# Two 64-row matmul passes in place of the last tail pass of the gate chain and of the up chain

## The chip, the cores and the metric

The kernel runs on one NeuronCore of a Trainium2 chip. The metric is the device time of one execution in microseconds. Inside the core five engines work from queues of their own: TensorE (PE in the profile, with its weight loads as PEld), VectorE (DVE), ScalarE (ACT), GpSimd (POOL) and SyncE (SP). PE, DVE and ACT each take their instructions strictly in the order in which the program wrote them, and wait on each other through semaphores. Matmuls read SBUF and write PSUM; ScalarE and VectorE read PSUM.

## The reference

The inputs are a matrix x of 2048 tokens by 576 features and the weights of two branches. A gate per token mixes the branches.

```python
g = sigmoid((x * gate_w).sum(-1, keepdims=True))
a = irfft2(rfft2(x) * (w_r + 1j * w_i))               # spectral branch, 2048 x 576
b = (gelu(x @ w_gate) * (x @ w_up)) @ w_down          # GEGLU branch, 576 -> 4608 -> 576
out = g * a + (1 - g) * b
```

All is float32. The kernel gets float32 accuracy out of faster matmuls by splitting each operand in a high part of 12 bits of mantissa and a low part, the rest. A product is then three passes: high by high, low weights by high x, high weights by low x.

## The kernel before, in words

**Two streams of work.** The GEGLU branch is the stream that feeds TensorE. The spectral branch is a long list of VectorE and ScalarE work (Python generators in the list `gens`), of which a piece is written into the program at every call of `gap()`, as far as a credit allows; `tick(us)` raises the credit by the time of the matmuls just written. So the order on each engine is fixed when the program is built.

**Slots.** In the first part of the program, tokens come in blocks of 512 (`tb`), and the 4608 hidden features in 36 tiles of 128 (`j`). A slot is one pair of hidden tiles for one token block: `hidden(j)`, then two calls of `down` for the slot before, then `hidden(j + 1)`, whose `mid` holds the other two calls of `down`. The next slot starts with its `hidden` at once; nothing is written on PE between the second `hidden` of a slot and the first `hidden` of the next.

**One hidden tile.** `hidden` calls `chain` twice: the gate chain into one PSUM buffer, then the up chain into the other. `pgu` is the name of these buffers, and `ps_gu()` hands out two of them in turn, so every gate chain uses the same buffer as the gate chain before it. A chain is 14 matmuls of 128 rows by 512 columns. The 576 features are four full blocks of 128 (three passes each, L728 to L730, from `xhi` and `xlo`) and a tail of 64. The tail's weights stand twice in the 128 rows; in `xtl` rows 0 to 63 hold the high part of the tail of x and rows 64 to 127 the low part, so L734 (high weights) does high by high and high by low in one pass, and L735 (low weights) does low by high and low by low.

After the gate chain ScalarE computes the GELU out of PSUM (L766, into `gl`), while PE runs the up chain. Then VectorE multiplies by the up chain's PSUM (L770), ScalarE makes the high part of the hidden tile (`hb`, L213) and VectorE the low part (L775). `down` reads `hb` a slot later with 128 by 288 matmuls (L789); ScalarE empties their PSUM (`pdn`) into `stg` (L814), and a DMA adds it to `yd`.

**The start.** The first hidden tile is written by `first_chains` (L747), which follows the arrival of x and the weights; the GELU after it is L763. `prep_x(tb, 4, src)` makes `xtl`: a ScalarE copy, then two VectorE steps (`stacked`, L217 and L218), the first of which overwrites `src`.

Of the kernel before, what the change touches and what calls it, by code (L numbers as in the profile page):

```python
# [10 lines left out]
F32 = mybir.dt.float32  # L11
F32R = mybir.dt.float32r
AF = mybir.ActivationFunctionType
ALU = mybir.AluOpType

P = 128
# [9 lines left out]
TB = 512  # L26
# [132 lines left out]
def _build(nc, tc, a):  # L159
    with ExitStack() as ctx:  # L160
        ctx.enter_context(tc.manual_schedule())
        pool = ctx.enter_context(tc.tile_pool(name="sb", bufs=1))
# [5 lines left out]
        def mk(n, shape, dt=F32):  # L168
            return pool.tile([P] + shape, dt, name=n, tag=n)
# [13 lines left out]
        raw = [raws[:, i * (KT * 256 + D):(i + 1) * (KT * 256 + D)] for i in range(2)]  # L183
        hb = [mk(f"hb{i}", [2, TB], F32R) for i in range(3)]
        gl = [mk(f"gl{i}", [TB]) for i in range(2)]
        xraw = mk("xraw", [4, TB])
        stg = [mk(f"stg{i}", [2, HD]) for i in range(4)]
        gs = mk("gs", [NB])
        gate = mk("gate", [NB])
# [22 lines left out]
        def copy(o, i):  # L212
            act.activation(o, i, AF.Copy)  # L213

        def stacked(o, x):

            vec.tensor_scalar(x, x, msk[:, 1:2], None, op0=ALU.mult)  # L217
            vec.scalar_tensor_tensor(o, f(o), msk[:, 0:1], x, op0=ALU.mult, op1=ALU.add)  # L218
# [11 lines left out]
        def columns():  # L230
# [4 lines left out]
            sgn = tmp[:, 3 * SW:3 * SW + NK]  # L235
            turn = [d + 4 * q for d in range(4) for q in range(4)]
            Z = [st[q] for q in turn]
            flat = xraw.rearrange("p q k -> p (q k)")
            sp, gw, xg = flat[:, 0:SW], flat[:, SW:SW + D], flat[:, 1280:1280 + D]
            xh2, xl2, vs2 = two(xh), two(xl), two(vs)  # L240

# [162 lines left out]
        def first_tiles(h):  # L404

            sp = tmp[:, 0:2 * SW].rearrange("p (e k) -> p e k", e=2)
            tmps = [tmp[:, SW * i:SW * (i + 1)] for i in range(4)]
            tmps = [(x, x[:, 0:NK], x[:, NK:]) for x in tmps]
            e = slice(2 * h, 2 * h + 2)
            yield from _butterfly(vec, lambda i: T[:, i, e], lambda i: T[:, i, e, re], lambda i: T[:, i, e, im],  # L410
                                  TAKEN, sp, -1, (1.37, 0.76))
            places = [((k, TAKEN[o]), o * k) for k in range(1, 4) for o in range(1, 4) if TAKEN[o] // 2 == h]
            yield from _twiddles(vec, act, lambda d, e: T[:, d, e], lambda d, e: T[:, d, e, re],
                                 lambda d, e: T[:, d, e, im], places, tmps, -1, 0.5)
            yield None
# [181 lines left out]
        def spectral(rows):  # L597
            yield from forward_rows(0, rows)
            rows = rows_tile()
            load_rows(rows, 1)  # L600
            zero_pads(0)
            yield None
            yield from first_tiles(0)
            yield None
            zero_pads(1)
            yield from forward_rows(1, rows)
            for _ in range(3):
                yield None
            yield from first_tiles(1)
            yield from columns()  # L610
            yield from last_tiles()
            for h in range(2):
                yield from inverse_rows(h)
# [3 lines left out]
        aux = []  # L617
        later = []
        gens = []
        side = []  # L620
        credit = [0.0]
        count = [0]

        def tick(us):
            credit[0] += RATE * us
# [52 lines left out]
        def prep_x(tb, k, src):  # L678
            if k < 4:
                copy(xhi[tb][:, k], src)  # L680
                vec.tensor_tensor(xlo[tb][:, k], src, f(xhi[tb][:, k]), ALU.subtract)
                credit[0] -= 0.7
            else:
                copy(xtl[tb], src)
                stacked(xtl[tb], src)
                credit[0] -= 1.45

# [32 lines left out]
            copy(g[:, 0], r)  # L720
            lower(("dn", j), g, r, 0.76)

        def chain(j, s, tb):
            due(("gu", j))
            ps, w = ps_gu(), gu[j % 3]
            c = slice(s * P, (s + 1) * P)
            for k in range(4):
                pe.matmul(ps, w[:, 0, k, c], xhi[tb][:, k], start=k == 0, stop=False)  # L728
                pe.matmul(ps, w[:, 1, k, c], xhi[tb][:, k], start=False, stop=False)  # L729
                pe.matmul(ps, w[:, 0, k, c], xlo[tb][:, k], start=False, stop=False)  # L730
                tick(3 * 0.2265)
                if k in (0, 2):
                    gap()
            pe.matmul(ps, w[:, 0, 4, c], xtl[tb], start=False, stop=False)  # L734
            pe.matmul(ps, w[:, 1, 4, c], xtl[tb], start=False, stop=True)  # L735
            tick(2 * 0.2265)
            return ps

        def first_chains():

# [15 lines left out]
        def hidden(j, tb, mid):  # L756

            i = hn[0]
            hn[0] += 1
            g, h = gl[i % 2], hb[i % 3]  # L760
            if i == 0:
                pg, pu = first_chains()
                act.activation(g, pg, AF.Gelu_apprx_tanh)  # L763
            else:
                pg = chain(j, 0, tb)
                act.activation(g, pg, AF.Gelu_apprx_tanh)  # L766
                mid()
                pu = chain(j, 1, tb)
            def mult():
                vec.tensor_tensor(g, g, pu, ALU.mult)  # L770
                credit[0] -= 0.7
                copy(h[:, 0], g)

            def low():
                vec.tensor_tensor(h[:, 1], g, f(h[:, 0]), ALU.subtract)  # L775
                credit[0] -= 0.7

            seq(("h", i), (1, mult), (3, low))
            return h, ("h", i)
# [86 lines left out]

        def load_xs(i):
            for q in range(4):
                nc.sync.dma_start(xraw[:, q], a["xs"][q // 2, q % 2][:, i])

        def operands():

            sx = pool.tile([P, 16 * SW], F32R, name="sx", tag="til")
            s4 = pool.tile([P, 2 * UNIT], F32R, name="s4", tag="tmp")
            parts = [sx[:, 2048 * i:2048 * (i + 1)].rearrange("p (l t k) -> p l t k", l=2, t=2) for i in range(3)]
            parts.append(s4[:, 0:2048].rearrange("p (l t k) -> p l t k", l=2, t=2))
            tails = [sx[:, 6144 + TB * i:6144 + TB * (i + 1)] for i in range(6)] + [s4[:, 2048:2560]]
            for i in range(4):
                ops["s1 s2 s3 s4".split()[i]] = (parts[i][:, 0], parts[i][:, 1], tails[i])
            ops["a11"] = (xhi[0][:, 0:2], xlo[0][:, 0:2], tails[4])  # L880
            ops["a12"] = (xhi[0][:, 2:4], xlo[0][:, 2:4], tails[5])
            ops["a22"] = (xhi[1][:, 2:4], xlo[1][:, 2:4], tails[6])
            m = misc[:, 0:TB]
            for i in range(3):
                if i:
                    load_xs(i)
                    for _ in range(6):
                        yield None
                a11, a12, a21, a22 = (xraw[:, q] for q in range(4))
                if i == 2:  # L890
                    for n, x in (("a11", a11), ("a12", a12), ("a22", a22)):
                        tail_of(ops[n][2], x)
                        yield 1.4
                        yield None
                for o, x, z, op in ((m, a21, a22, ALU.add), (a21, a11, a21, ALU.subtract),
                                    (a11, m, a11, ALU.subtract), (a12, a12, a11, ALU.subtract)):
                    vec.tensor_tensor(o, x, z, op)
                    yield 0.72
                sums = (("s1", m), ("s2", a11), ("s3", a21), ("s4", a12))
                yield None  # L900
                if i == 2:
                    for n, x in sums:
                        tail_of(ops[n][2], x)
                        yield 1.4
                        yield None
                else:
                    for n, x in sums:
                        copy(ops[n][0][:, i], x)
                    yield None
                    yield None  # L910
                    for n, x in sums:
                        vec.tensor_tensor(ops[n][1][:, i], x, f(ops[n][0][:, i]), ALU.subtract)
                        yield 0.72
            ops["done"] = True
# [58 lines left out]
        def products(i, spare, pend):  # L973

            j = NT + 2 * i
            u, c, u3 = gl, [xraw[:, q] for q in range(2)], [xraw[:, q] for q in range(2, 4)]
            made = {}

            def finish(name, x):
# [102 lines left out]
        ps = ps_gu()  # L1082
# [32 lines left out]
        def load_x(i):  # L1115
            if i < 2 * KT:
                tb, k = divmod(i, KT)
                nc.sync.dma_start(xraw[:, i % 4], a["xt"][1][:, k, tb * TB:(tb + 1) * TB])

        def reload_x(tb):  # L1120
            for k in range(KT):
                i = KT * tb + k
                aux.append(lambda i=i, k=k: [prep_x(tb, k, xraw[:, i % 4]), load_x(i + 4)])

        NBLK = NT // 2
        prev = None
# [124 lines left out]
```

## Time and profile before

| what | value |
|---|---|
| median of 3 runs | 1380.88 us (1380.46 to 1381.74) |
| the profiled execution, its own time | 1381.8 us |
| its span, first to last instruction | 1380.0 us |
| PE busy | 1370.2 us, 99% of the span |
| DVE, ACT, POOL busy | 1108.8, 687.1 and 269.6 us |
| mean granted TensorE clock | 0.999 |

The profile is one execution. Its page gives for each engine the busy time, groups of instructions by source line, the digits of 40 slices of the span, and the chain of work that ended last. Other views list instructions in order of time (start, duration, engine, line, operation, tiles; in brackets the idle time of the engine just before, and what ended it), or the busy time in chosen stretches. A matmul's row shows 0.39 us for a 512-column pass although the next begins 0.22 to 0.23 us later: passes are pipelined, and the start-to-start distance is what one costs.

### The profile page before, as it was taken

How to read it: one execution, taken by the hardware profiler on the slowest of the kernel's cores; microseconds unless marked ns; L12 is line 12 of the kernel's file. 1: busy time of each engine (PE TensorE's matmuls, PEld its weight loads, DVE VectorE, ACT ScalarE, POOL GpSimd, SP SyncE). 2: the span in 40 equal slices, each digit the busy share in tenths (PEclk: the TensorE clock that was granted, in tenths of full speed). 3: DMA queues.
4: the chain of work that ended last, by engine and by line, in shares of the span. 5: the costliest groups of instructions: out<-in, count | busy, mean ns of one | idle time of the engine just before them, and what ended most of it. 6: DMA issues, size and time to landing. Idle time of an engine off the chain costs nothing.

```text
span 1380.0 us, 19978 instructions
## 1 busy us (share of the span) xinstructions
PE 1370.2 (99%) x7518; PEld 1211.3 (88%) x7518; DVE 1108.8 (80%) x1628; ACT 687.1 (50%) x1051; POOL 269.6 (20%) x326
## 2 busy tenths in 40 slices
PE   8999999999999999999999999999999999999998
PEld 6888888888888898888888888888888888888887
DVE  5999789888968787678989898857877777777776
ACT  4553443544465565554354634375555555555552
POOL 0022121222222222211111311232111111111110
PEclk9999999999999999999999999999999999999999
DMA  7466676666899999765675576687677777776776
GB/s 265 143 124 112 122 158 122 115 111 139 205 224 261 234 230 243 145 121 105 143 149 137 120 155 138 111 207 152 126 130 131 129 130 130 130 128 128 131 155 172
DMA packets 97041, 210.91 MB, mean 153 GB/s; under 512 B 11824, under 2 KB 22064, under 8 KB 96560
## 3 DMA queue, kind: packets, MB, share of 16 engines
q0 software_dynamic: 45248, 92.56, 44.0%
q1 hardware_dynamic: 51696, 117.08, 27.6%
q8 instruction: 59, 0.97, 0.3%
q14 instruction: 38, 0.31, 0.1%
HBM read 110.43 MB, written 92.01 MB: 147 GB/s over the span
## 4 chain that ended last, share of the span: by engine, by line
PE 96%; DVE 2%; DMA 1%; issue 0%; ACT 0%; SPq 0%; DVEq 0%
PE pdn L789 32%; PE pgu L728 12%; PE pgu L730 12%; PE pgu L729 12%; PE pgu L966 3%; PE pgu L968 3%; PE pgu L967 3%; PE pgu L735 3%; PE pgu L734 3%; PE pone L966 2%; PE pone L968 2%; PE pone L967 2%; PE pf L275 2%; PE pgu L969 2%; PE pone L969 1%; DVE tmp L661 1%
## 5 line engine op out<-in xcount | busy, mean ns | idle before, releaser
L802 POOL DMA_DIRECT2D yd<-stg x264 | 230.9, 878 | 996.5 <-ACT stg L814 880.6
L789 PEld LDWEIGHTS pdn<-dn,hb 128*128 128x128 f32 x2856 | 395.0, 188 | 11.6 <-DVE raws L843 0.5
L789 PE MATMUL pdn<-dn,hb 128*128 128x288 f32 x2856 | 403.1, 295 | 0.2 <-DVE raws L843 0.2
L814 ACT ACTIVATE stg<-pdn,omg 128x576 f32<-128x576 f32 x272 | 201.6, 743 | 402.4 <-PE pdn L789 312.6
L728 PE MATMUL pgu<-xhi,gu 128*128 128x512 f32 x760 | 297.8, 392 | 2.7 <-ACT gl L763 2.1
L730 PE MATMUL pgu<-xlo,gu 128*128 128x512 f32 x760 | 297.1, 391 | 0.0
L729 PE MATMUL pgu<-xhi,gu 128*128 128x512 f32 x760 | 296.9, 391 | 0.0
L730 PEld LDWEIGHTS pgu<-xlo,gu 128*128 128x128 f32 x760 | 143.0, 188 | 31.1
L728 PEld LDWEIGHTS pgu<-xhi,gu 128*128 128x128 f32 x760 | 143.1, 188 | 29.9 <-ACT gl L763 2.5
L729 PEld LDWEIGHTS pgu<-xhi,gu 128*128 128x128 f32 x760 | 143.0, 188 | 25.7
L770 DVE TENSOR_TENSOR gl<-gl,pgu 128x512 f32<-128x512 f32 x96 | 65.8, 685 | 73.1 <-PE pgu L735 72.6
L213 ACT ACTIVATE hb<-gl 128x512 fp32r<-128x512 f32 x96 | 60.2, 627 | 114.1 <-DVE gl L770 114.0
L766 ACT ACTIVATE gl<-pgu 128x512 f32<-128x512 f32 x95 | 56.8, 598 | 90.9 <-PE pgu L735 90.8
L213 ACT ACTIVATE gu<-raws 128x1280 fp32r<-128x1280 f32 (+3 forms) x83 | 87.0, 1048 | 5.0 <-DMA raws<-wgu 4.8
L775 DVE TENSOR_TENSOR hb<-gl,hb 128x512 fp32r<-128x512 f32 x96 | 65.9, 686 | 18.4 <-ACT hb L213 18.3
L789 PEld LDWEIGHTS pdn<-dn,gu 128*128 128x128 f32 x576 | 79.0, 188 | 1.8
L789 PE MATMUL pdn<-dn,gu 128*128 128x288 f32 x576 | 80.1, 295 | 0.0
L735 PE MATMUL pgu<-xtl,gu 128*128 128x512 f32 x190 | 74.0, 389 | 0.0
L734 PE MATMUL pgu<-xtl,gu 128*128 128x512 f32 x190 | 73.9, 389 | 0.0
L708 DVE TENSOR_TENSOR gu<-raws,gu 128x1280 fp32r<-128x1280 f32 x46 | 68.3, 1484 | 3.9 <-ACT gu L213 3.8
L708 DVE TENSOR_TENSOR dn<-raws,dn 128x576 fp32r<-128x576 f32 x72 | 54.1, 751 | 1.3 <-ACT dn L213 1.3
L984 DVE TENSOR_TENSOR xraw<-xraw 128x512 f32<-128x512 f32 x48 | 33.2, 693 | 26.4 <-ACT xraw L992 25.9
(213 smaller groups left out, 2109.9 us busy)
## 6 DMA issues: line engine op xcount, KB each, us to landing
yd<-stg POOLq DMA_DIRECT2D x264, 288.0 KB, 5.1
raws<-wgu SPq DMA_DIRECT2D x46, 640.0 KB, 5.0
raws<-wd SPq DMA_DIRECT2D x72, 288.0 KB, 2.8
colm<-col POOLq DMA_DIRECT2D x32, 256.0 KB, 6.1
quads<-ws SPq DMA_DIRECT2D x20, 384.0 KB, 4.6
raws<-ws SPq DMA_DIRECT2D x18, 384.0 KB, 4.8
tmp<-wf SPq DMA_DIRECT2D x16, 290.0 KB, 5.8
cns<-til SPq DMA_DIRECT2D x64, 72.5 KB, 5.2
```

Of the source, the lines that this page charges most:

```text
L213: act.activation(o, i, AF.Copy)
L708: vec.tensor_tensor(g[:, 1], r, f(g[:, 0]), ALU.subtract)
L728: pe.matmul(ps, w[:, 0, k, c], xhi[tb][:, k], start=k == 0, stop=False)
L729: pe.matmul(ps, w[:, 1, k, c], xhi[tb][:, k], start=False, stop=False)
L730: pe.matmul(ps, w[:, 0, k, c], xlo[tb][:, k], start=False, stop=False)
L734: pe.matmul(ps, w[:, 0, 4, c], xtl[tb], start=False, stop=False)
L735: pe.matmul(ps, w[:, 1, 4, c], xtl[tb], start=False, stop=True)
L789: pe.matmul(ps[half], h[:, l, c], d[:, q, half * HD:(half + 1) * HD], start=part == 0 and n == 0, stop=part == 1 and n == 2)
L802: pl.dma_start(yd[u], o, accum_op=ALU.add)
L814: put(u, lambda o: act.activation(o.rearrange("p (c k) -> p c k", c=2), v[:, :, 0:HD], AF.Copy, scale=omg[:, u:u + 1]), i == 0)
L966: pe.matmul(ps, hi[:, c], xh[:, t], start=t == 0, stop=False)
L967: pe.matmul(ps, lo[:, c], xh[:, t], start=False, stop=False)
```

## The change

While a flag `twin` is set, both chains leave out their last pass (the low tail weights). When the up chain is done, `last_halves` writes two matmuls of 64 rows each: rows 0 to 63 of the low tail weights of the gate, with the high part of x in rows 0 to 63 of `xtl`, into the gate's PSUM buffer; and rows 64 to 127 of the low tail weights of the up projection, with a copy of the high part of x in rows 64 to 127 of a new tile `xth`, into the up buffer. The two use different rows of the array and different PSUM buffers. The products of low weights by low x, which L735 also computed, are left out where the flag is set.

The GELU is now written after these two passes, because the gate's PSUM sum is complete only then. `prep_x` gets one more ScalarE copy (64 rows) for each of the two token blocks. The credit of a chain is smaller by half a pass. `xth` takes the memory of `xraw`, which is allocated later, at the start of `columns`. The flag is cleared when the spectral stream reaches `first_tiles(1)`. In the built program the new line (L750 of the changed file) stands 66 times: 33 hidden tiles have it, the second tile of the first slot and both tiles of the 16 slots after that; 17 of these are the second tile of a slot and 16 the first.

```diff
@@ prep_x
                 copy(xtl[tb], src)
+                if twin[0]:
+                    copy(xth[64:128, tb], src[64:128])
                 stacked(xtl[tb], src)
@@ chain
-        def chain(j, s, tb):
+        def chain(j, s, tb, whole):
...
             pe.matmul(ps, w[:, 0, 4, c], xtl[tb], start=False, stop=False)
-            pe.matmul(ps, w[:, 1, 4, c], xtl[tb], start=False, stop=True)
-            tick(2 * 0.2265)
+            if whole:
+                pe.matmul(ps, w[:, 1, 4, c], xtl[tb], start=False, stop=True)
+            tick((1.5 + 0.5 * whole) * 0.2265)
             return ps
+
+        def last_halves(j, tb, ps):
+
+            for s, x in enumerate((xtl[tb], xth[:, tb])):
+                r = slice(64 * s, 64 * s + 64)
+                pe.matmul(ps[s], gu[j % 3][r, 1, 4, s * P:(s + 1) * P], x[r], start=False, stop=True)
@@ hidden
-                pg = chain(j, 0, tb)
-                act.activation(g, pg, AF.Gelu_apprx_tanh)
+                halves = twin[0]
+                pg = chain(j, 0, tb, not halves)
+                if not halves:
+                    act.activation(g, pg, AF.Gelu_apprx_tanh)
                 mid()
-                pu = chain(j, 1, tb)
+                pu = chain(j, 1, tb, not halves)
+                if halves:
+                    last_halves(j, tb, (pg, pu))
+                    act.activation(g, pg, AF.Gelu_apprx_tanh)
+
@@ spectral
+            twin[0] = False
             yield from first_tiles(1)
```

Two places show what moves. The first is PE at the end of a slot's second hidden tile and the start of the next slot. `xtl_71` and `xtl_70` are the tails of the two token blocks, `gu_75` and `gu_76` two buffers of split gate and up weights; the brackets name the engine whose semaphore the instruction waits on. Before:

```order
L730 MATMUL pgu<-xlo_69,gu_75 128x512
L734 MATMUL pgu<-xtl_71,gu_75 128x512
L735 MATMUL pgu<-xtl_71,gu_75 128x512
L728 MATMUL pgu<-xhi_66,gu_76 128x512 [waits Activation_49]
L729 MATMUL pgu<-xhi_66,gu_76 128x512 [waits DVE_49]
```

And with the change:

```order
L736 MATMUL pgu<-xlo_69,gu_75 128x512
L740 MATMUL pgu<-xtl_71,gu_75 128x512
L750 MATMUL pgu<-xtl_71,gu_75 128x512
L750 MATMUL pgu<-xth,gu_75 128x512
L734 MATMUL pgu<-xhi_66,gu_76 128x512 [waits Activation_49]
L735 MATMUL pgu<-xhi_66,gu_76 128x512 [waits DVE_49]
```

The next slot's first matmul (L728, now L734) waits for ScalarE in both. It writes the gate's PSUM buffer, so it waits for the GELU that reads that buffer.

The second place is ScalarE around the same spot, one slot further on: `gl_86` is the output of the GELU of a slot's second hidden tile, `gl_85` that of the next slot's first, `stg_90` and `stg_91` are the outputs of the two `down` calls of `mid`. Before:

```order
L766 ACTIVATE gl_86<-pgu 128x512
L814 ACTIVATE stg_90<-pdn,omg 128x576
L814 ACTIVATE stg_91<-pdn,omg 128x576
L213 ACTIVATE dn_78<-raws 128x576
L213 ACTIVATE hb_83<-gl_86 128x512
L766 ACTIVATE gl_85<-pgu 128x512
```

And with the change:

```order
L833 ACTIVATE stg_90<-pdn,omg 128x576
L833 ACTIVATE stg_91<-pdn,omg 128x576
L786 ACTIVATE gl_86<-pgu 128x512
L214 ACTIVATE dn_78<-raws 128x576
L214 ACTIVATE hb_83<-gl_86 128x512
L786 ACTIVATE gl_85<-pgu 128x512
```

The GELU of the second tile moved behind the two evictions of `mid`; the copies after it kept their places.

More of the change, by code (lines that the diff above doesn't have):

```diff
@@ L185, in _build @@
         gl = [mk(f"gl{i}", [TB]) for i in range(2)]
-        xraw = mk("xraw", [4, TB])
+        xth = pool.tile([P, 4, TB], F32R, name="xth", tag="xraw")
+        late = []
         stg = [mk(f"stg{i}", [2, HD]) for i in range(4)]
@@ L237, in columns @@
             Z = [st[q] for q in turn]
-            flat = xraw.rearrange("p q k -> p (q k)")
+            late.append(pool.tile([P, 4, TB], F32, name="xraw", tag="xraw"))
+            flat = late[0].rearrange("p q k -> p (q k)")
             sp, gw, xg = flat[:, 0:SW], flat[:, SW:SW + D], flat[:, 1280:1280 + D]
@@ L620, in _build @@
         side = []
+        twin = [True]
         credit = [0.0]
@@ L868, in load_xs @@
             for q in range(4):
-                nc.sync.dma_start(xraw[:, q], a["xs"][q // 2, q % 2][:, i])
+                nc.sync.dma_start(late[0][:, q], a["xs"][q // 2, q % 2][:, i])
         def operands():
@@ L888, in operands @@
                         yield None
-                a11, a12, a21, a22 = (xraw[:, q] for q in range(4))
+                a11, a12, a21, a22 = (late[0][:, q] for q in range(4))
                 if i == 2:
@@ L975, in products @@
             j = NT + 2 * i
-            u, c, u3 = gl, [xraw[:, q] for q in range(2)], [xraw[:, q] for q in range(2, 4)]
+            u, c, u3 = gl, [late[0][:, q] for q in range(2)], [late[0][:, q] for q in range(2, 4)]
             made = {}
@@ L1117, in load_x @@
                 tb, k = divmod(i, KT)
-                nc.sync.dma_start(xraw[:, i % 4], a["xt"][1][:, k, tb * TB:(tb + 1) * TB])
+                nc.sync.dma_start(late[0][:, i % 4], a["xt"][1][:, k, tb * TB:(tb + 1) * TB])
         def reload_x(tb):
@@ L1122, in reload_x @@
                 i = KT * tb + k
-                aux.append(lambda i=i, k=k: [prep_x(tb, k, xraw[:, i % 4]), load_x(i + 4)])
+                aux.append(lambda i=i, k=k: [prep_x(tb, k, late[0][:, i % 4]), load_x(i + 4)])
         NBLK = NT // 2
```

## The prediction

> **What bounds the kernel now.** I read the page first: its header, the busy shares, the 40 slices and the chain that ended last.
>
> ```profile
> span 1380.0 us, 19978 instructions
> PE 1370.2 (99%) x7518; PEld 1211.3 (88%) x7518; DVE 1108.8 (80%) x1628; ACT 687.1 (50%) x1051; POOL 269.6 (20%) x326
> PE 96%; DVE 2%; DMA 1%; issue 0%; ACT 0%; SPq 0%; DVEq 0%
> ```
>
> TensorE has work for 99% of the span and makes up 96% of the chain, so time comes and goes with what stands in its queue. Next, the busy time by stage, for the stretch in which the changed slots lie: after the start, up to 333 us.
>
> ```profile
> core 0: us, PE busy (x) PEld busy (x) DVE busy (x) ACT busy (x) POOL busy (x), PEclk, DMA share, GB/s
> 70.00:333.00 263.00, 263.00 (x1432) 232.18 (x1431) 232.09 (x300) 117.95 (x186) 50.66 (x59) 1.00 0.64 123
> ```
>
> Here PE has no gap at all in 263 us, at the full clock. A pass that goes saves its whole pitch, and a wait that comes is paid in full: nothing in this stretch lets PE catch up. Then the order of time on PE, for the price of one pass and for the seam between two slots:
>
> ```profile
> 19.52 0.39 PE L735 MATMUL pgu<-xtl,gu 128*128 128x512 f32 x1
> 25.87 0.39 PE L735 MATMUL pgu<-xtl,gu 128*128 128x512 f32 x1
> ...
> 118.82 0.39 PE L735 MATMUL pgu<-xtl,gu 128*128 128x512 f32 x1
> 119.04 0.39 PE L728 MATMUL pgu<-xhi,gu 128*128 128x512 f32 x1
> ```
>
> The first two rows are 28 passes apart (two chains of 14): 6.35 / 28 = 0.227 us a pass. The last two are the end of an up chain at a slot's second tile and the next slot's gate chain, 0.22 us later: the seam costs nothing, because the GELU that frees the gate's PSUM buffer has run a whole up chain earlier. Last, ScalarE around that seam:
>
> ```profile
> 116.69 0.68 ACT L213 ACTIVATE dn<-raws 128x576 fp32r<-128x576 f32 x1
> 120.03 0.64 ACT L213 ACTIVATE hb<-gl 128x512 fp32r<-128x512 f32 x1 [2.67 <-DVE gl L770]
> ```
>
> ScalarE is idle from 117.4 to 120.0 us; a GELU written there starts as soon as its PSUM sum is complete.
>
> **The change part by part.** *Passes removed.* 66 passes of 0.227 us go, 15.0 us; 66 half passes come. If the two of a pair run at the same time, 33 × 0.227 = 7.5 us are saved; if they run one after the other, nothing.
>
> *The wait at the seam.* This is the large term. The GELU now follows the pair, and where the pair ends a slot's second tile, the very next matmul writes the buffer that this GELU reads. With two buffers in turn there is no other. The start of the program shows the same situation, a GELU (L763) with PE behind it, and two ordinary GELUs show how soon one starts:
>
> ```profile
> 14.22 0.58 ACT L763 ACTIVATE gl<-pgu 128x512 f32<-128x512 f32 x1
> 14.85 0.50 PE L728 MATMUL pgu<-xhi,gu 128*128 128x512 f32 x1 [2.05 <-ACT gl L763]
> 15.19 0.54 PE L729 MATMUL pgu<-xhi,gu 128*128 128x512 f32 x1
> ...
> 19.95 0.60 ACT L766 ACTIVATE gl<-pgu 128x512 f32<-128x512 f32 x1 [2.61 <-PE pgu L735]
> 26.36 0.60 ACT L766 ACTIVATE gl<-pgu 128x512 f32<-128x512 f32 x1 [1.31 <-PE pgu L735]
> ```
>
> From the start of a chain's last pass to the GELU's start: 19.95 - 19.52 = 0.43 and 26.36 - 25.87 = 0.49, mean 0.46 us. The GELU takes 0.60. From its end to PE's restart: 14.85 - (14.22 + 0.58) = 0.05. So the next gate chain starts 0.46 + 0.60 + 0.05 = 1.11 us after the pair's first half, where a pass allows 0.227: a wait of 0.88 us. The first pitch after such a wait is longer too, 15.19 - 14.85 = 0.34, 0.11 more than a pass. With one pass saved: 0.88 + 0.11 - 0.227 = +0.77 us at each of 17 seams, 13.0 us. It hardly matters here whether the halves overlap, since the GELU hangs on the first half alone. Lower end, without the 0.11: 11.2 us.
>
> *The 16 first tiles of a slot.* After their pair come two calls of `down`, 24 matmuls into other PSUM buffers, so their GELU is hidden behind 24 × 0.131 = 3.1 us; it delays PE only if it comes more than that late. What the pair costs is not in this trace: every matmul in it uses 128 rows. Bounds: 0.227 (full overlap) and 0.454 (none). The nearest row is the densest train of weight loads, `down`, where each matmul brings its own load:
>
> ```profile
> 125.39 1.08 PE L789 MATMUL pdn<-dn,hb 128*128 128x288 f32 x7
> L789 PE MATMUL pdn<-dn,hb 128*128 128x288 f32 x2856 | 403.1, 295 | 0.2 <-DVE raws L843 0.2
> ```
>
> Seven of them in 1.08 us, the last 0.295 long, make (1.08 - 0.295) / 6 = 0.131 us each, so two loads for the halves take 0.26 us. I take a pair at 0.262: it is nearer full overlap, since the halves share neither rows nor buffers. That saves 0.454 - 0.262 = 0.192 us in 16 places, -3.1 us; ends -3.6 and 0. The Trainium skill (TensorE: Matmul & The Clock Gate, "The mechanism" in Part 3) says that matmuls on different row groups start about 4 ns apart and run together. By it a pair would cost 0.231 us, this term -3.6 and the sum +9.4; no run here shows it yet.
>
> *VectorE.* Its multiply (L770) waits for the GELU, now some 0.7 us after the up chain. At a seam PE waits as long. At a first tile only VectorE does, 0.7 us a slot. A slot is 56 × 0.227 + 48 × 0.131 = 19.0 us, so the stage above holds 13.8 of them and VectorE idles (263.00 - 232.09) / 13.8 = 2.2 us in each: covered. Without that cover 16 × 0.7 = 11 us would land on PE by way of `hb`. The smaller credit moves spectral work a little later; from some way behind the flag's end on, the order on every engine is the same again.
>
> *The start.* The 64-row copy into `xth` must end before L217 overwrites its source; at most it takes as long as the 128-row copy of the same width, 0.62 us, and it delays the tail passes of `first_chains` by that. But behind them PE waits 2.05 us for L763, which stands behind copies that wait for a DMA:
>
> ```profile
> 9.56 0.62 ACT L213 ACTIVATE xtl<-til 128x512 fp32r<-128x512 f32 x1
> 13.06 1.25 ACT L213 ACTIVATE xhi<-til 128x512 fp32r<-128x512 f32 x2 [0.25 <-DMA til<-xt]
> 12.00:15.40 3.40, 1.35 (x6) 0.82 (x5) 3.23 (x5) 2.48 (x4) 0.00 (x0) 0.98 1.01 367
> 15.50:18.90 3.40, 3.40 (x10) 2.68 (x9) 2.03 (x4) 1.67 (x3) 0.00 (x0) 0.53 1.10 383
> ```
>
> So it costs nothing; +0.6 if the cover were gone. The last row shows 3.4 us at a granted clock of 0.53 behind that wait, 1.6 us lost. With 0.6 us of the idle time filled this might not happen: -1.6 at best. I take 0. The second copy runs beside passes that do not need it.
>
> *One odd slot*, where ScalarE is late already:
>
> ```profile
> 58.53 1.28 ACT L766 ACT_TABLE_LOAD   x1
> 62.05 2.12 ACT L823 ACTIVATE til<-til,omg 128x576 f32<-128x576 f32 x3
> 64.08 0.39 PE L735 MATMUL pgu<-xtl,gu 128*128 128x512 f32 x1
> 64.76 0.50 PE L728 MATMUL pgu<-xhi,gu 128*128 128x512 f32 x1 [0.29 <-DVE gl L770]
> ```
>
> PE loses 0.68 - 0.227 = 0.45 us there now, and 0.11 after. That wait goes, but the GELU at this seam comes behind the three copies, up to 2 us late. Ends -0.6 and +2; I take 0.
>
> *Sum:* 13.0 - 3.1 = +9.9 us, of which the skill's rule would make 9.4. The profiled execution took 1381.8 us, 1.8 around its span; its span would become 1389.9 and its time 1391.7. The median of the runs lies 0.9 below it, at 1380.88, which gives **1390.8 us**.
>
> **The rivals.** *A, the halves do not overlap, or the switch to half rows costs.* Without overlap the 3.1 us are not saved: 1393.9. If PE also runs empty at each switch, a row's 0.389 us less the pitch is 0.16 us, once before each pair and once more after the 16 that have no wait behind them: 33 × 0.16 + 16 × 0.16 = 7.8, 1401.7. For it: no row shows any half-row matmul. Against: nothing ties the halves together. A page of the Trainium skill speaks for the second part (TensorEngine Tiling (Array Packing), "Key Properties"): changing the tiling mode drains TensorE. No trace so far bears on that rule.
>
> *B, the GELU is late on ScalarE.* Its new place is behind both evictions of `mid` and whatever the spectral stream put in the up chain's gaps. If one more copy of 0.7 us stood in front at each seam, 17 × 0.7 = 12 us: 1402.7. Against: the idle 2.67 us in the ScalarE rows. For: the odd slot.
>
> *C, the clock falls at every seam.* As after the 2.05 us wait: 17 × 1.6 = 27 us, 1418. Against: the wait of 0.45 us at 64.08 was followed by a full clock:
>
> ```profile
> 63.00:69.00 6.00, 5.71 (x29) 4.56 (x28) 5.90 (x13) 2.85 (x5) 0.00 (x0) 1.00 0.78 272
> ```
>
> 0.88 us is nearer that one.
>
> *D, not slower: no wait at the seam.* If the gate chain could start before the GELU is done, only the saving stays: 33 × 0.227 = 7.5 us less, 1373.4. It decides from the point where the GELU has 1.11 us of other PE work behind it. Against: on PE's order nothing stands between the pair and the next gate chain, and its first matmul waits on ScalarE, as L728 did at 14.85.
>
> **How the numbers follow.** Forecast 62%, A 22%, B 7%, C 4%, D 5%. Its own unknowns give the forecast 11.2 - 3.6 - 1.6 - 0.6 = +5.4 to 13.0 + 0.6 + 2 = +15.6 with no overlap, 1386 to 1396. To hold 8 in 10 the range takes in most of A: 1386 to 1399. This kernel's measurements tell 0.2% (2.8 us) from no change. All cases but D lie above that: slower 95%, faster 4%, the same 1%.
>
> **What would show it.** The next gate chain (L734) starting about 1.1 us after the pair's first half, released by the GELU, 17 times (as idle time some 0.7 us, since a matmul's row reaches 0.16 us past its pitch): the large term. The two rows of L750 starting nearly together, or 0.2 us apart: overlap or A. A GELU that starts later than 0.5 us after the first half: B. A granted clock under 1 between 70 and 333 us: C. Gate chains 0.23 us behind the pair: D. The forecast is wrong if the 17 seams, start to start, cost under 10 or over 19 us, or if time comes up behind 350 us.

## The result

The changed kernel takes 1403.8 us (median of 4 runs, 1403.42 to 1404.20), the kernel before 1380.67 us (4 runs). The ratio is 1.0167, with a 95% interval of 1.0149 to 1.0184: 23 us slower, where 10 us slower was forecast and 1386 to 1399 us was the range. The direction was right, the size was not. Of all executions below one, of the kernel with the two copies alone, took 2775.3 us where the ten others took 1379.7 to 1382.5 us; its ratio leaves that execution out, and no row of it is used.

The page of the changed kernel, in the lines that answer to those of before: the span, the busy shares and the group of the first matmuls of a block, with that group's line from the page of before behind it.

```profile
span 1401.6 us, 19989 instructions
PE 1379.0 (98%) x7518; PEld 1203.6 (86%) x7518; DVE 1110.2 (79%) x1628; ACT 688.3 (49%) x1053; POOL 268.5 (19%) x326
L734 PE MATMUL pgu<-xhi,gu 128*128 128x512 f32 x760 | 299.1, 394 | 15.2 <-ACT gl L786 12.8
...
L728 PE MATMUL pgu<-xhi,gu 128*128 128x512 f32 x760 | 297.8, 392 | 2.7 <-ACT gl L763 2.1
```

The number of matmuls is the same, 7518, and the idle time ahead of L734 (L728 before) has grown from 2.7 to 15.2 us, 12.8 of it ended by the GELU. The busy times by stage, for the stretch that had no gap:

```profile
70.00:333.00 263.00, 251.34 (x1338) 210.07 (x1337) 215.21 (x279) 108.83 (x170) 47.50 (x55) 1.00 0.60 114
```

PE is idle for 11.7 of 263 us, at the full clock, and gets 1338 matmuls done there instead of 1432. So most of the time is lost in the changed slots. One seam, from the views in order of time of PE and of ScalarE:

```profile
121.86 0.39 PE L736 MATMUL pgu<-xlo,gu 128*128 128x512 f32 x1
122.09 0.39 PE L740 MATMUL pgu<-xtl,gu 128*128 128x512 f32 x1
122.41 0.50 PE L750 MATMUL pgu<-xtl,gu 64*128 64x512 f32 x1
122.41 0.50 PE L750 MATMUL pgu<-xth,gu 64*128 64x512 f32 x1
123.59 0.50 PE L734 MATMUL pgu<-xhi,gu 128*128 128x512 f32 x1 [0.69 <-ACT gl L786]
123.93 0.39 PE L735 MATMUL pgu<-xhi,gu 128*128 128x512 f32 x1
...
122.94 0.60 ACT L786 ACTIVATE gl<-pgu 128x512 f32<-128x512 f32 x1 [2.65 <-PE pgu L750]
```

The two halves start together. The GELU follows 0.53 us later, takes 0.60, and the next gate chain starts 1.18 us behind the pair: the seam wait. The pitch ahead of the pair is 122.41 - 122.09 = 0.32 us, not 0.23. At a first tile of a slot, where no GELU is waited for, there is a second surprise (PE, and PEld, its weight loads):

```profile
129.40 0.39 PE L740 MATMUL pgu<-xtl,gu 128*128 128x512 f32 x1
129.71 0.50 PE L750 MATMUL pgu<-xtl,gu 64*128 64x512 f32 x1
129.72 0.50 PE L750 MATMUL pgu<-xth,gu 64*128 64x512 f32 x1
130.15 1.06 PE L808 MATMUL pdn<-dn,hb 128*128 128x288 f32 x6
...
129.17 0.19 PEld L740 LDWEIGHTS pgu<-xtl,gu 128*128 128x128 f32 x1
129.71 0.18 PEld L750 LDWEIGHTS pgu<-xtl,gu 64*128 64x128 f32 x1 [0.35 <-issue]
129.72 0.18 PEld L750 LDWEIGHTS pgu<-xth,gu 64*128 64x128 f32 x1
130.14 0.96 PEld L808 LDWEIGHTS pdn<-dn,hb 128*128 128x128 f32 x7 [0.25 <-issue]
```

`down` starts 0.43 us behind the pair. An ordinary weight load runs ahead: L740's load begins at 129.17, with the matmul before it. The load of a half and the load of L808 begin only with their own matmul.

**Where the time went.** From the start-to-start distances of all matmuls, less the pitch of their shape (0.227, 0.131 and 0.133 us; a pair counted as one pass), the two profiled executions differ by:

| what | us |
|---|---|
| 33 passes fewer, 0.227 each | -7.5 |
| going into a pair, 33 times 0.09 | +3.0 |
| pair to the next gate chain (seam), 17 times, mean 1.03 | +17.4 |
| pair to `down` (first tiles), 16 times 0.20 | +3.2 |
| longer pitch of 0.11 behind a wait or a pair, 38 times instead of 3 | +3.9 |
| other waits, 3.6 instead of 1.3 | +2.2 |
| the first 19.7 us | -1.6 |
| small differences | +1.0 |
| sum (1401.6 - 1380.0) | +21.6 |

The other waits and the start are not in the changed passes. The largest of the waits is 1.8 us at 187 us, where an up chain waits for VectorE's multiply. VectorE and GpSimd there, and GpSimd at the same work before the change:

```profile
183.13 1.37 DVE L93 TENSOR_TENSOR tmp<-til 128x1160 f32<-128x1160 f32 x1 [1.78 <-POOL til L597]
184.53 4.17 DVE L93 TENSOR_TENSOR til<-til 128x1160 f32<-128x1160 f32 x3
188.62 0.68 DVE L789 TENSOR_TENSOR gl<-gl,pgu 128x512 f32<-128x512 f32 x1
...
180.74 1.76 POOL L821 DMA_DIRECT2D yd<-stg  x2 [2.26 <-ACT til L513]
182.51 0.58 POOL L597 MEMSET til<- 128x16 f32 x1
...
169.28 0.46 POOL L595 MEMSET til<- 128x16 f32 x1
172.80 0.86 POOL L802 DMA_DIRECT2D yd<-stg  x1 [3.06 <-ACT stg L814]
174.40 0.86 POOL L802 DMA_DIRECT2D yd<-stg  x1 [0.73 <-ACT stg L814]
```

A zero fill of the spectral tile (L597) stands on GpSimd behind two DMA issues that wait for evictions; before the change it stood ahead of them (L595). VectorE waits for it and then works off four long steps ahead of the multiply. What moved it is the smaller credit per chain, as the runs further down show.

### The profile page after: what moved, and what is told of

It reads as the page before. It is cut to its first block, busy times and chain, and to the rows that moved or that the text cites. A ratio compares the mean times of both kernels' runs of the same rounds, so it can differ in the third digit from the quotient of the medians.

```text
span 1401.6 us, 19989 instructions
## 1 busy us (share of the span) xinstructions
PE 1379.0 (98%) x7518; PEld 1203.6 (86%) x7518; DVE 1110.2 (79%) x1628; ACT 688.3 (49%) x1053; POOL 268.5 (19%) x326
## 4 chain that ended last, share of the span: by engine, by line
PE 71%; issue 18%; DVE 3%; POOL 3%; DMA 2%; ACT 1%; SPq 0%; POOLq 0%; DVEq 0%; ACTq 0%
PE pdn L808 24%; PE pgu L734 8%; PE pgu L735 7%; PE pgu L736 7%; PE pgu L985 3%; PE pgu L987 3%; PE pgu L986 3%; POOL yd L821 3%; PE pone L986 2%; PE pone L987 2%; PE pone L985 2%; PE pgu L740 2%; PE pf L277 2%; PE pgu L988 2%; PE pgu L742 1%
## 5 line engine op out<-in xcount | busy, mean ns | idle before, releaser
L808 PEld LDWEIGHTS pdn<-dn,hb 128*128 128x128 f32 x2856 | 393.8, 188 | 14.2 <-issue 3.9
L808 PE MATMUL pdn<-dn,hb 128*128 128x288 f32 x2856 | 404.9, 296 | 0.2 <-DVE raws L862 0.2
L734 PE MATMUL pgu<-xhi,gu 128*128 128x512 f32 x760 | 299.1, 394 | 15.2 <-ACT gl L786 12.8
L735 PE MATMUL pgu<-xhi,gu 128*128 128x512 f32 x760 | 296.6, 390 | 0.0
L734 PEld LDWEIGHTS pgu<-xhi,gu 128*128 128x128 f32 x760 | 142.7, 188 | 47.1 <-ACT gl L786 18.2
L735 PEld LDWEIGHTS pgu<-xhi,gu 128*128 128x128 f32 x760 | 142.7, 188 | 25.1
L808 PEld LDWEIGHTS pdn<-dn,gu 128*128 128x128 f32 x576 | 79.0, 188 | 1.8
L808 PE MATMUL pdn<-dn,gu 128*128 128x288 f32 x576 | 80.1, 295 | 0.0
L740 PE MATMUL pgu<-xtl,gu 128*128 128x512 f32 x190 | 73.9, 389 | 0.0
L786 ACT ACTIVATE gl<-pgu 128x512 f32<-128x512 f32 x33 | 19.7, 597 | 109.7 <-PE pgu L750 109.7
```

What stands on the lines that cost most here:

```text
L808: pe.matmul(ps[half], h[:, l, c], d[:, q, half * HD:(half + 1) * HD], start=part == 0 and n == 0, stop=part == 1 and n == 2)
```

## The experiments

The theory formed from these rows, S: the loss is the seam wait plus a price for every change between 128-row and half-row matmuls. Each rival is named in the expectation that tests it.

**The wait without half rows.** Both last passes whole, in the pair's place; this adds low weights by low x again, as before the change.

```diff
-            for s, x in enumerate((xtl[tb], xth[:, tb])):
-                r = slice(64 * s, 64 * s + 64)
-                pe.matmul(ps[s], gu[j % 3][r, 1, 4, s * P:(s + 1) * P], x[r], start=False, stop=True)
+            for s in range(2):
+                pe.matmul(ps[s], gu[j % 3][:, 1, 4, s * P:(s + 1) * P], xtl[tb], start=False, stop=True)
```

> The changed kernel, but in the pair's place stand the two last passes over all 128 rows (as before the change, only later), the GELU still behind them. No half-row matmul is left. Theory S (the loss is two things: a seam wait for the GELU, and a price for every change between 128-row and half-row matmuls): the seam wait alone stays. The GELU starts after the first of the two passes, so a seam costs 1.11 + 0.11 - 2 x 0.227 = about +0.77 us, 17 times +13 us, first tiles of a slot cost nothing; with what the changed spectral order adds (0 to 3 us) 1393 to 1397 us. Rival P (the half-row passes bring all of the loss, the wait for the GELU lies beside it): 1381 us. Rival O (the shifted order of VectorE and ScalarE work makes the loss): 1400 us or more.

Measured: 1400.1 us (ratio 1.0140, 1.0125 to 1.0155). The seams were as expected, 0.62 to 0.71 us from the second pass to the next gate chain above a pass, and 0.11 behind it. Rival P, which puts all of the loss on half rows, falls. But the whole is 3 us above the expected range, and the rows show where outside the seams: a VectorE wait of 2.0 us at 185 us, a stretch of half clock behind it, a late GELU of 1.4 us at 264 us, and 1.0 us at 966 us. Part of rival O is true.

**The pairs without the wait.** The second tile of a slot takes the spectral PSUM buffers, idle in this stage.

```diff
-        def chain(j, s, tb, whole):
+        def chain(j, s, tb, whole, ps=None):
...
+                own = ps_f2() if halves and i % 2 else None
+                own = (None, None) if own is None else (own[:, 0], own[:, 1])
-                pg = chain(j, 0, tb, not halves)
+                pg = chain(j, 0, tb, not halves, own[0])
...
-                pu = chain(j, 1, tb, not halves)
+                pu = chain(j, 1, tb, not halves, own[1])
```

> The changed kernel, but the second tile of a slot sums its gate and up chains in the two PSUM buffers that the spectral branch uses only later; the first tile keeps the two old ones. So the next slot's gate chain has not to wait for the GELU of the tile just ended. Theory S: the seam wait is gone, the price of the switch stays: each pair 0.09 us going in, 0.20 and 0.11 going out on top of 0.227, where two whole passes cost 0.454, so +0.18 us for 33 pairs = +6 us, with up to 2 us either way from start and order: 1384 to 1389 us. Rival W (only the wait costs, the 0.09, 0.20 and 0.11 are shadows of it): pairs save 0.227 each, 1373 us. Rival P: 1400 us or more.

Measured: 1387.6 us (1.0052, 1.0037 to 1.0067). A seam of this kernel on PE:

```profile
136.81 0.39 PE L740 MATMUL pf<-xtl,gu 128*128 128x512 f32 x1
137.12 0.50 PE L750 MATMUL pf<-xtl,gu 64*128 64x512 f32 x1
137.13 0.50 PE L750 MATMUL pf<-xth,gu 64*128 64x512 f32 x1
137.55 0.50 PE L734 MATMUL pgu<-xhi,gu 128*128 128x512 f32 x1
137.89 0.40 PE L735 MATMUL pgu<-xhi,gu 128*128 128x512 f32 x1
```

No wait for the GELU, and the price is there all the same: 0.31 into the pair, 0.43 out of it, 0.34 for the pass behind, where passes of 0.227 stand elsewhere. From L740 to L735 it is 1.08 us against 3 × 0.227 = 0.68 for a pair that cost one pass, so 0.40 on top; a pair costs 0.63 us and two whole passes 0.45. Rival W falls: the price is no shadow of the wait.

**Is it the half rows or the change to them?** Every pair twice.

```diff
-            for s, x in enumerate((xtl[tb], xth[:, tb])):
...
-                pe.matmul(ps[s], gu[j % 3][r, 1, 4, s * P:(s + 1) * P], x[r], start=False, stop=True)
+            for n in range(2):
+                for s, x in enumerate((xtl[tb], xth[:, tb])):
...
+                    pe.matmul(ps[s], gu[j % 3][r, 1, 4, s * P:(s + 1) * P], x[r], start=False, stop=n == 1)
```

> The changed kernel with every pair written twice in a row (gate half, up half, gate half, up half), so that the low-weight tail products are counted twice in the output. Theory S (a price for the change of the number of rows, in the matmul that follows a change): the second pair follows the first after one pass, 0.22 to 0.23 us, and the gaps before the first and after the second are those of the single pair (0.32 us from the last whole pass to the first half, 0.43 us from the last half to the next whole matmul at first tiles): about 33 x 0.23 = 7.5 us more than the changed kernel, 1410 to 1412 us. Rival H (a half-row pass is slow by itself, since its weight load is not hidden): the second pair follows after 0.32 us or more, 1414 us or above.

Measured: 1412.5 us (2 runs; 1.0232, 1.0211 to 1.0252), 8.7 us over the changed kernel and half a microsecond above the range of S. PE and PEld at a first tile:

```profile
132.48 0.39 PE L740 MATMUL pgu<-xtl,gu 128*128 128x512 f32 x1
132.79 0.49 PE L751 MATMUL pgu<-xtl,gu 64*128 64x512 f32 x1
132.80 0.49 PE L751 MATMUL pgu<-xth,gu 64*128 64x512 f32 x1
133.13 0.39 PE L751 MATMUL pgu<-xtl,gu 64*128 64x512 f32 x1
133.13 0.39 PE L751 MATMUL pgu<-xth,gu 64*128 64x512 f32 x1
133.46 0.40 PE L809 MATMUL pdn<-dn,hb 128*128 128x288 f32 x1
...
132.79 0.18 PEld L751 LDWEIGHTS pgu<-xtl,gu 64*128 64x128 f32 x1 [0.35 <-issue]
132.80 0.18 PEld L751 LDWEIGHTS pgu<-xth,gu 64*128 64x128 f32 x1
132.90 0.19 PEld L751 LDWEIGHTS pgu<-xtl,gu 64*128 64x128 f32 x1
132.91 0.19 PEld L751 LDWEIGHTS pgu<-xth,gu 64*128 64x128 f32 x1
133.45 0.30 PEld L809 LDWEIGHTS pdn<-dn,hb 128*128 128x128 f32 x2 [0.36 <-issue]
```

The second pair follows after 0.33 us, which at first sight is rival H. The loads tell it apart: the second pair's loads begin at 132.90, 0.11 us behind the first pair's and 0.23 us before their own matmuls, so within half rows loads do run ahead. The extra 0.11 belongs to the first pair, whose load was not hidden; and the way out has become 0.33 (133.13 to 133.46), 0.10 less than the 0.43 behind a single pair, because the 0.11 is no longer in it. From L740 to the first `down` matmul it is 0.98 us here and 0.75 us in the changed kernel: the second pair cost 0.23 us, one pass. S holds, with a sharper reading: at each change the load of the new kind starts 0.09 us later than a pass's pitch, and the pitch behind it is longer by 0.11 us, which is the step from that load to the next one (132.79 to 132.90). The two changes make 0.40 us, with one pair between them or with two. 33 times 0.23 is 7.6 us; the rest of the 8.7 us lies outside the pairs, in other waits and in the start.

**The side effects alone.** Old passes, old place of the GELU; left are the two copies, the shared memory and the smaller credit.

```diff
-            if whole:
-                pe.matmul(ps, w[:, 1, 4, c], xtl[tb], start=False, stop=True)
+            pe.matmul(ps, w[:, 1, 4, c], xtl[tb], start=False, stop=True)
...
-                if not halves:
-                    act.activation(g, pg, AF.Gelu_apprx_tanh)
+                act.activation(g, pg, AF.Gelu_apprx_tanh)
...
-                if halves:
-                    last_halves(j, tb, (pg, pu))
-                    act.activation(g, pg, AF.Gelu_apprx_tanh)
```

> The kernel before, with the side effects of the change alone: the copies into the second tail tile, the memory it shares, and the smaller credit that shifts spectral work; all last passes whole and in their old place, the GELU behind the gate chain. Theory S: within 2 us of the kernel before, 1379 to 1383 us, since PE has neither the wait nor the switch; a VectorE wait as at 187 us of the changed kernel (1.8 us) may show. Rival O (the shifted order costs): 1385 us or more.

Measured: 1386.1 us (1.0044, 1.0028 to 1.0061; single runs 1384.9 to 1387.7). My own expectation failed; rival O holds. PE waits 3.0 us for the multiply at 178 us, where VectorE's first long step again waits for the zero fill, and 1.1 us at 951 us.

**Which side effect?** The same kernel with the old credit:

```diff
-            tick((1.5 + 0.5 * whole) * 0.2265)
+            tick(2 * 0.2265)
```

> The kernel before with the two copies into the second tail tile and the shared memory, nothing else. Theory S+O: the copies are hidden and the order is the old one: 1380.5 us, within 0.7 us. Rival (the copies or the shared memory, not the credit, cost what the order-only kernel lost): 1384 us or more.

Measured: 1380.8 us (0.9998, 0.9989 to 1.0007). The copies and the shared memory cost nothing; the credit, by the order that it sets, cost 5.3 us (1386.1 less 1380.8).

**The three kernels with the old credit.** The same line was changed in the changed kernel, in the one with more PSUM buffers, and in the one with whole passes late. With the old order the flag is cleared one tile earlier: 32 pairs and 16 seams.

> The changed kernel with the credit of the kernel before, so that spectral work stands in the slots where it stood. Theory S+O (seam wait, switch price, and about 4 to 5 us because the smaller credit put the zero fill of a spectral tile on GpSimd behind two more DMA issues and moved other VectorE work against the chains): what is left is 17 seams at about 0.97 us and 16 first tiles at 0.18 us, 19.4 us less the 0.6 us of the odd slot, over 1380.5: 1398 to 1400 us, and no wait of 1 us or more on VectorE between 150 and 220 us. Rival: the order costs only in combination with whole passes: 1403 us or more.

> Two more PSUM buffers for the second tile of a slot, and the credit of the kernel before: the switch price alone. Theory S+O: 33 pairs at +0.18 us, 5.9 us over 1380.5: 1385.5 to 1387 us. Rival (the 7 us of the run with more PSUM buffers was order, and pairs save as hoped): under 1380 us.

> Whole last passes at the end of the up chain with the GELU behind them, and the credit of the kernel before: the seam wait alone. The run with the smaller credit showed 0.62 to 0.68 us more from the last pass to the next gate chain, and 0.11 us behind it. Theory S+O: 17 x 0.77 = 13.1 us, less 0.6 us of the odd slot, over 1380.5: 1392 to 1394.5 us. Rival (late GELUs upset VectorE and ScalarE whatever the credit): 1398 us or more.

| | smaller credit | old credit | ratio, old credit |
|---|---|---|---|
| the change | 1403.8 | 1399.1 | 1.0133 (1.0119 to 1.0147) |
| more PSUM (switch price alone) | 1387.6 | 1384.3 | 1.0025 (1.0015 to 1.0035) |
| whole passes late (seam wait alone) | 1400.1 | 1394.4 | 1.0096 (1.0083 to 1.0110) |
| neither | 1386.1 | 1380.8 | 0.9998 (0.9989 to 1.0007) |

The smaller credit costs 3.3 to 5.7 us in every row; in the first row about 1 us of its 4.7 is the one seam more, not order (an estimate: a seam of the changed kernel cost 1.0 us more than before the change). With the old credit the change and the whole passes late came out in their expected ranges. The seam wait alone costs 13.7 us, the switch price alone 3.7, together 17.4 of the 18.5 that the change costs with the old credit. The 3.7 is less than the expected 5.9: in the profile of that run, 3.1 us over that of before, the 32 pairs lose 5.6 us, but 2.4 us are won back in the first 19.7 us, and 0.6 at the odd slot's wait that is gone. The seam of the kernel with whole passes, free of other effects (PE, then ScalarE):

```profile
121.98 0.61 PE L749 MATMUL pgu<-xtl,gu 128*128 128x512 f32 x2
123.05 0.50 PE L734 MATMUL pgu<-xhi,gu 128*128 128x512 f32 x1 [0.46 <-ACT gl L785]
...
122.40 0.60 ACT L785 ACTIVATE gl<-pgu 128x512 f32<-128x512 f32 x1 [2.46 <-PE pgu L749]
```

From the first pass to the next gate chain: 123.05 - 121.98 = 1.07 us, forecast as 1.11.

**Covering the seam by order.** Old credit, and `mid` behind the second tile's pair, so that 24 `down` matmuls stand there.

```diff
-                mid()
+                if not halves:
+                    mid()
...
                     act.activation(g, pg, AF.Gelu_apprx_tanh)
+                    mid()
```

> The changed kernel with the credit of the kernel before, and with the two down calls that stand between the gate and the up chain of a slot's second tile written behind its pair instead. So 24 matmuls (3.1 us) lie between the pair and the next slot's gate chain, more than the 1.2 us that the GELU needs. Theory S+O: the seam wait is covered by order alone, the switch price stays as in the run with two more PSUM buffers and the old order (1384.3): 1383 to 1386 us. Rival (the new place makes another wait, on the evictions or on VectorE's multiply): 1388 us or more.

Measured: 1395.0 us (1.0100, 1.0085 to 1.0115). The seam wait is gone (one is left, at 23 us in the first slot, which has no `down` to put there), but new waits took its place, as the rival said:

```profile
PE pgu L734 <- DVE gl L791: 4.7, 4, 1.8
PE pgu L734 <- ACT gl L787: 0.7, 1, 0.7
```

Between 20 and 350 us up chains wait four times for VectorE's multiply, 4.7 us, where the kernel before waits once, 0.3 us. The pairs still pay their price, 32 of the 33 now with the 0.20 us out to `down`. In the wait at 185 us the GELU has ended at 180.1 us, and VectorE runs other steps without a gap from 180.05 us to the multiply at 186.94 us: it is late for work that stands ahead of the multiply in its order. Against the run with more PSUM and the old credit, 5.6 us more are such waits and 3.2 us come in the first 19.7 us, where this profile has 3.4 us of half clock and that one none.

**The zero fill on VectorE.** The changed kernel, smaller credit included.

```diff
-            pl.memset(til.rearrange("p (t k) -> p t k", k=NK)[:, 16 * h:16 * h + 16, KF:], 0.0)
+            vec.memset(til.rearrange("p (t k) -> p t k", k=NK)[:, 16 * h:16 * h + 16, KF:], 0.0)
```

> The changed kernel, smaller credit and all, but the zero fill of the spectral tile is done by VectorE and not by GpSimd. If the part of the order's loss at 187 us comes from the zero fill standing behind two DMA issues on GpSimd, the wait of the up chain there (1.8 us, and 0.1 behind it) goes: 1401 to 1402.5 us. Rival (VectorE is late there for its own work): 1403 to 1404 us.

Measured: 1403.3 us (1.0161, 1.0145 to 1.0178). The wait at 187 us shrank from 1.78 to 0.13 us, so its cause is the zero fill. The total is what the rival said, though its reason, VectorE's own work, is not what the rows show: it hardly moved, and the profiled execution shows 3.8 us of waits between 963 and 977 us, where the changed kernel has 1.0 (start to start, above a pass). That execution took 1406.3 us, 3.0 us over the median of this kernel, so these waits need not stand for the other executions. Why the median did not fall by the 1.7 us stays open.

## Why the prediction was wrong

In the two profiled executions the change costs 21.6 us where the sum was 9.9. Of the 11.7 us between them, the pairs at the first tiles are 5.9, the seams 4.0, the other waits and small differences 3.4, and the start takes 1.6 back.

**What bounds the kernel: right.** PE had no slack in the stage, and every wait was paid in full.

**The seam wait: right in kind and nearly in size.** Forecast +0.77 us each, 13.0 us; alone, in the kernel with whole passes late and the old credit, it cost 13.7 us for 16 seams, one of them with a GELU 1.2 us late, and 1.07 us where 1.11 was forecast. In the changed kernel the seams came to 17.0 us, inside the 10 to 19 us named for them: 1.5 of it is the 0.09 us going into 17 pairs, and the GELU started 0.53 to 0.60 us behind the half pass instead of 0.46. One GELU, at 267.5 us, started 1.16 us behind it, after other ScalarE work (rival B, once).

**The pair: the step that failed most.** I took 0.262 us, by the pitch of weight loads in `down`, and argued "it is nearer full overlap, since the halves share neither rows nor buffers". The overlap is full: the two start within 5 ns. What the sum put at nothing, and left to rival A, was the change of rows. A pair costs 0.227 + 0.40 = 0.63 us, more than the 0.454 that it replaces. So the first tiles brought +2.8 us, not -3.1 (16 × (0.63 - 0.454)). The row that I used was from a train in which all loads are of one kind and run ahead; it could not bound a load that does not. Rival A, with 22%, had the mechanism, but its 0.16 us per switch was too little against 0.20 (0.09 and 0.11). That its time, 1401.7, was near the result is in part luck: it held 3.1 us for halves that do not overlap, which did not come, and neither the 4.0 us at the seams nor the order.

The Trainium skill (TensorEngine Tiling (Array Packing), "Key Properties") says that changing the tiling mode drains TensorE. The trace agrees in that each change costs 0.20 us; that TensorE runs empty is not shown, for the pair at 122.41 us begins before the row of the pass ahead of it ends (122.09 + 0.39). The other rule of the Trainium skill that I weighed (TensorE: Matmul & The Clock Gate, "The mechanism" in Part 3) is that matmuls on different row groups start about 4 ns apart. The trace agrees: 129.714 and 129.717 us by the records, 3 ns.

**The order: costed at nothing, and wrong.** I wrote that the smaller credit "moves spectral work a little later", and that the order is the same again behind. In between, the zero fill fell behind two DMA issues. The credit cost 4.7 us (1403.8 less 1399.1, about 1 of it the one seam more), and none of the rivals held it. The wait for the zero fill is 1.8 us of this; what makes the rest was not separated, and with the fill on VectorE the median fell by only 0.5 us. To see the fill, GpSimd's order would have had to be compared at that place, as PE's and ScalarE's were.

**The odd slot: misread.** The wait at 64.76 us is no seam. The seam of that slot lies at 61.14 us, 0.23 us behind the pass before it; at 64.76 us the up chain of the slot's first tile waits for VectorE's multiply of the tile before. With the change that wait is gone, 0.6 us, and the GELU at that seam came in time, 0.53 us behind its half pass, so nothing of the 2 us came.

**The start: right in cost, not in size.** The copies are hidden: alone they cost nothing (1380.8 us). The profiled execution of before, 1381.8 us, contains the half-clock stretch and is 1.1 us above its median, while the changed kernel's profile has no such stretch. So the spans differ by 21.6 us and the medians by 23.1.

**Rivals C and D fell:** the clock stood at 1.00 over the stage, and no seam was free. No version that I ran beats the kernel before.

## What to carry to other kernels

Two half-row matmuls side by side save a pass only if several pairs share one change to half rows and back. Here the way in and out cost 0.40 us, nearly two passes of 0.227, so one pair lost. By an estimate from these two numbers two pairs would about break even; four PSUM sums would have to stay open at once for them, and no run here tried it. Before moving the last write of a PSUM sum later, count what stands between its reader and the next write into that buffer; with nothing between, the reader's whole latency (1.1 to 1.2 us here) is paid each time. A planner's estimate is part of a change: shifting it by 0.2 us a tile moved work on other engines, a tiny fill on GpSimd among it, and cost 3 to 6 us.

## What the runs showed of the hardware

A weight load of another number of rows does not run ahead of the passes before it: ordinary loads begin with the preceding matmul, 0.23 us early; at a change they begin with their own, 0.32 us after the start of the preceding 512-column pass. Within half rows, loads run ahead again.

Not every long wait brings the half clock. In the kernel with whole passes late and the smaller credit, a wait of 2.0 us at 185 us was followed by it:

```profile
184.00:188.00 4.00, 2.18 (x10) 1.48 (x9) 3.97 (x5) 0.63 (x1) 0.00 (x0) 1.00 0.98 313
188.10:191.50 3.40, 3.40 (x10) 2.65 (x9) 2.95 (x5) 0.00 (x0) 0.00 (x0) 0.50 0.92 234
```

Waits of 1.8 us at 187 us (the change), of 3.0 us at 178 us (the side effects alone) and of 2.0 us at 185 us (`mid` behind the pair) were not: the granted clock behind them is 1.00.
